# Gated linear attention and a squared-ReLU layer on one core: later chunks of 128 tokens handled in pairs

## The chip, the core and the metric

The kernel runs on one core of a Trainium2 chip. A core has a matrix engine (TensorE, PE in the profile, with its weight loads as PEld), VectorE (DVE), ScalarE (ACT), GpSimd (POOL) and SyncE (SP), which here only issues transfers, and 16 DMA engines. Each engine works through its own queue in order. PE and its helpers exchange data through PSUM (eight banks of 2 KB per partition) and SBUF. The metric is the device time of one execution in microseconds. The span in a profile runs from the first to the last instruction; the time of the execution is a little longer.

## The reference

```python
# q, k, v, alpha: (4, 8, 768, 48); w_in (384, 2048); w_out (2048, 384)
for t in range(S):
    state = alpha[:, :, t, :, None] * state + np.einsum('bhd,bhe->bhde', k[:, :, t], v[:, :, t])
    y[:, :, t] = np.einsum('bhd,bhde->bhe', q[:, :, t], state)
x = np.ascontiguousarray(y.transpose(0, 2, 1, 3)).reshape(B * S, H * D)      # 3072 x 384
h = x @ w_in
r = np.maximum(h, 0.0)
out = (r * r) @ w_out
```

## The kernel before

**Chunks.** The recurrence is computed in 24 chunks of 128 tokens, six to each of the four batch entries. With A the running product of alpha inside a chunk, a chunk needs the scores (q A)(k / A)^T under a triangular mask, the product of q A with the state that the chunks before left, and the new state. All eight heads of a chunk are worked on together, two heads (2 x 48 channels, padded to 2 x 64) on the 128 partitions.

**One chunk's steps.** ScalarE takes the logarithm of alpha (L396, tile L_s). PE sums it along the tokens with a triangular matrix (p0), ScalarE takes exponentials of the sum and of its negative. For chunks before number 11 DVE multiplies q and k by these in token order (L502, L505), PE transposes both products, and a copy brings them to SBUF. From chunk RAW = 11 on ("raw" chunks) the plain q and k are cast to bf16 on POOL (L413, tile rawb) and transposed by a DMA (L416, DMA_TRANSPOSE, tile rawt), one for q and one for k of each chunk, each over four blocks of 128 columns. PE then forms the running sum in transposed form too (pT, four matmuls L_s by the triangular matrix), ScalarE's exponentials of it (L451 into qkT, L454 into aiT) are multiplied by the transposed q and k on DVE (L507, L510). Then come the scores on PE (p2, tile sc: eight matmuls of 64 rows, two heads side by side in the two halves of the array), two masks on DVE (L561), the product with v and with the state (p3a, p3b), a cast on ScalarE (xn, L386), and a transpose of the chunk's output into xT_big (by PE and DVE, for chunks 18 to 22 by a DMA, L620).

**Feed-forward.** Tokens are taken in groups (4, 1, 1 and then nine groups of 2 chunks). The first layer (add_moe1) fills a bank with 512 columns, ScalarE applies ReLU (L676, tile r, 96 in all), DVE squares (L684, tile gT). The second layer (add_moe2) accumulates over 16 blocks; its result is copied to an output tile and stored. The first eight token tiles are held in SBUF (tile keep) and stored late by two large transfers; tiles 8 to 17 are stored by transfers that POOL issues (L772), the rest by SP.

**Order.** The order of all work is written by a planner inside the kernel. Each operation is an `Op` with an engine, a planned duration, dependencies, a priority, and `lat`, the time from its end until its result counts as there. `Plan.run` picks greedily by planned times, and the instructions of all engines are emitted in that order, so each engine's queue is fixed when the program is built. Loads are planned on one line called DMA, one after the other; transposing DMAs ("TR") also take time on that line (TLD) and count as landed TLAT later, and their `late` moves their place in SP's queue back. All loads and transposing DMAs are issued from SP's queue. A chunk may begin when the feed-forward has progressed far enough (`gate`, with LEAD).

**PSUM.** The scores have two banks of their own (sl_sc, tile sc), the state has one, and five banks serve the rest. The small steps of the chunks use banks 0 and 1 (GLA_BANKS), the first layer banks 2 to 4, the second layer banks 4 to 2.

The helpers `mm` (L240) and `tr` (L243) record all matmuls and transposes, so these two lines stand for most of PE's work, and tiles tell the steps apart. A tile `bank` is any of the five banks.

Of the kernel before, what the change touches and what calls it, by code (L numbers as in the profile page):

```python
# [38 lines left out]
class Op:  # L39


    def __init__(self, eng, dur, emit, deps=(), prio=0.0, takes=None, gives=None, lat=None, at=0.0):
        self.eng, self.dur, self.emit = eng, dur, emit
        self.deps = []
        for d in deps:
            if d is not None:
                d = d if isinstance(d, tuple) else (d, None)
                if d[0] is not None:
                    self.deps.append(d)
        self.prio = prio  # L50
        self.takes, self.gives, self.lat, self.at = takes, gives, lat, at
        self.start = self.done = None

# [5 lines left out]
class Plan:  # L59
# [13 lines left out]
    def ready(self, op):  # L73
        t = op.at
        slack = PE_SLACK if "PE" in op.durs else 0.0
        if slack and self.free.get("PE", 0.0) > PE_CALM:
            slack = 0.25
        for d, x in op.deps:
            if d.done is None:
                return None  # L80
            if x is None:
                t = max(t, d.done + (slack if d.eng != "PE" else 0.0))
            else:
                t = max(t, d.start + d.dur + x)
        if op.takes is not None:
            best = None
            for sl in op.takes:
                f = sl.free_at()
                if f is not None and (best is None or f < best):
                    best, op.slot = f, sl  # L90
            if best is None:
                return None
            t = max(t, best)
        return t

    def run(self, gate):
        free = self.free
        while any(self.pending.values()):
# [34 lines left out]
            if op.takes is not None:  # L133
                self.ready(op)
                op.slot.release.append(op.gives if op.gives is not None else op)
            self.order.append(op)
            self.on_pick(op)
# [4 lines left out]
def kernel(  # L142
# [13 lines left out]
    P = 128  # L156
# [40 lines left out]
    utri_b = consts.tile([P, 1, P], BF16)  # L197
    nc.gpsimd.tensor_copy(utri_b[:, 0, :], utri_f)
    JN, JP = 4, 32
    JW = P + JN - 1  # L200
# [29 lines left out]
    nc.vector.memset(ae_s, 0.0)  # L230
    xT_big = big.tile([P, KT, n_tok], BF16)
    gT_s = big.tile([P, FT, 2 * P], BF16, name="gT2", tag="gT2")
# [78 lines left out]
    EARLY = 4  # L311
    RAW = 11
    XTURN = (18, 23)
    TLD, TLAT, TLATE = 1.0, 4.0, 2.0
    NR = 3
    R = {}

    def raw_tiles():
        if R:
            return  # L320
        R["b"] = stage.tile([P, NR, 2, H, DP], BF16, name="rawb", tag="stage")
        nc.gpsimd.memset(R["b"][:, :, :, :, D:], 0.0)
        R["t"] = stage.tile([P, NR, 2, NP, P], BF16, name="rawt", tag="stage")
        R["i"] = stage.tile([P, 2, NP, P], BF16, name="aiT", tag="stage")

# [38 lines left out]
    def add_load(s, nm):  # L364
        d = C[s]
        b, c = divmod(s, NCH)

        def ld():
            if nm not in d:
                d[nm] = loads.tile([P, H, D], FP32, name=nm)  # L370
            pin(nc.sync.dma_start(out=d[nm], in_=SRC[nm][b, c]))
        prev = C[s - LB].get("use_" + nm) if s >= LB else None
        d["ld_" + nm] = add("DMA", LD if s < 4 else LD1, ld, prev, lat=2.0 if s < 4 else LAG if s < 6 else 2.4, at=0.6)

    def add_chunk(s):
        d = C[s]
        b, c = divmod(s, NCH)
# [30 lines left out]
        if raw:  # L408
            w, wz = s % NR, s % 2

            def e_rb(j, nm):
                raw_tiles()
                pin(nc.gpsimd.tensor_copy(R["b"][:, w, j, :, 0:D], d[nm]))  # L413

            def e_turn(j):
                pin(nc.sync.dma_start_transpose(out=R["t"][:, w, j], in_=R["b"][:, w, j].rearrange("p h d -> p (h d)")))  # L416
            rt = []
            for j, nm in enumerate(["qt", "kt"]):
                cb = add("POOL", 0.55, lambda j=j, nm=nm: e_rb(j, nm), d["ld_" + nm],
                         *([C[s - NR]["turn"][j]] if s >= RAW + NR else []), prio=-5.0)  # L420
                d["use_" + nm] = cb
                t_ = add("TR", TLD, lambda j=j: e_turn(j), cb, *([C[s - NR]["turned"][j]] if s >= RAW + NR else []), lat=TLAT)
                t_.late = TLATE
                rt.append(t_)
            d["turn"] = rt
        vb = d["use_vt"] = add("POOL", 0.55, e_vb, d["ld_vt"], old, prio=-5.0)
# [22 lines left out]
        def e_AT():  # L449
            d["qkT"] = work.tile([P, 2 * NP, P], BF16, name="qkT")  # L450
            pin(nc.scalar.activation(d["qkT"][:, NP:2 * NP, :], d["pmT"], AF.Exp))  # L451

# [25 lines left out]
        if raw:  # L478
# [9 lines left out]
            aiT = add("ACT", 0.48, e_AiT, pT, after(aT), *([C[s - 2]["turned"][1]] if s >= RAW + 2 else []), **g)  # L488
            pT.gives = aiT
            if not last:  # L490
                ae0 = add("ACT", 0.18, lambda: e_aeT(0), pT, after(aiT), **g)
# [14 lines left out]
        def e_qAT():  # L506
            pin(nc.vector.tensor_mul(d["qkT"][:, 0:NP, :], R["t"][:, w, 0], d["qkT"][:, NP:2 * NP, :]))  # L507

        def e_kiT():
            pin(nc.vector.tensor_mul(d["qkT"][:, NP:2 * NP, :], R["t"][:, w, 1], R["i"][:, wz]))  # L510
        if raw:
            if not last:
                mk = d["use_kt"] = add("DVE", 0.47, e_kI, ai, d["ld_kt"], old, **g)
            cp = add("DVE", 0.34, e_qAT, aT, rt[0], **g)
            cpk = add("DVE", 0.34, e_kiT, aiT, rt[1], cp, **g)
            d["turned"] = [cp, cpk]
        else:
            mq = d["use_qt"] = add("DVE", 0.47, e_qA, a_, d["ld_qt"], old, **g)
            mk = d["use_kt"] = add("DVE", 0.47, e_kI, ai, d["ld_kt"], old, **g)

        def e_p1q():
# [26 lines left out]

        def e_p2():
            sc = d["sc"] = ps_sc.tile([P, 2, NP, P], FP32, name="sc")  # L550
            t = d["qkT"]
            for p in range(NP):
                for hh in range(2):
                    sl = slice(64 * hh, 64 * hh + 64)
                    mm(sc[:, hh, p, :], lhsT=t[sl, NP + p, :], rhs=t[sl, p, :], start=True, stop=True)
        p2 = d["p2"] = plan.add(Op("PE", 0.42, e_p2, [cp, cpk], takes=[sl_sc], lat=0.10, **g))

        def e_sm(hh):
            if hh == 0:
                d["sm"] = work.tile([P, 2, NP, P], BF16, name="sm")  # L560
            pin(nc.vector.tensor_mul(d["sm"][:, hh], d["sc"][:, hh], utri_b.to_broadcast([P, NP, P])))  # L561
        sm0 = add("DVE", 0.6, lambda: e_sm(0), p2, **g)
        sm1 = add("DVE", 0.6, lambda: e_sm(1), p2, after(sm0), **g)
        p2.gives = sm1

        if not last:
# [51 lines left out]
        if XTURN[0] <= s < XTURN[1]:  # L618
            def e_xt():
                pin(nc.sync.dma_start_transpose(out=xT_big[:, :, s * P:(s + 1) * P], in_=d["xn"]))  # L620
            d["x"] = add("TR", 0.8, e_xt, xn, lat=TLAT)
            d["x"].late = 1.0
            d["end"] = xn
# [3 lines left out]
        def e_xT():  # L627
            cast(xT, xT_big[:, :, s * P:(s + 1) * P], d["px"])
        xT = add({"ACT": 0.36, "DVE": 0.27} if s < EARLY else "DVE", 0.27, e_xT, p4, prio=-9.0)
# [13 lines left out]
    POOL_OUT = (5, 18)  # L643
    HELD, HELD_AT = 8, 150.0
    KEEP, held_ev = {}, []
# [6 lines left out]
    def add_moe1(g, f0, before, lo=0, hi=None, per=1):  # L652
        hi = GN[g] if hi is None else hi
        t0, n = (GT[g] + lo) * P, (hi - lo) * P
        w = per * n
# [18 lines left out]
        def e_relu():  # L674
            box["r"] = rpool.tile([P, 512], BF16, name="r")
            pin(nc.scalar.activation(box["r"][:, 0:w], box["ph"][:, 0:w], AF.Relu))  # L676
        rl = add("ACT", 0.055 + w / 1190.0, e_relu, op, prio=RELU_PRIO if g > 1 else RELU_PRIO0)
# [47 lines left out]
    def add_moe2(g, tt, before, box, quarters, pools):  # L725
# [22 lines left out]
        def e_ev():  # L748
            if held:
                if t % 4 == 0:  # L750
                    KEEP[t // 4] = stage.tile([P, 4, d_model], FP32, name="keep", tag="stage")
                box["ob"] = KEEP[t // 4][:, t % 4, :]
# [32 lines left out]
    for d in DMA_ORDER + list(range(6, NT)):  # L785
# [12 lines left out]
        else:  # L798
            for nm, _ in srcs:
                if nm != "at":  # L800
                    add_load(d, nm)
                elif d <= 9:
                    add_load(d, nm)
                if nm == "at" and 9 <= d < NT - 1:
                    add_load(d + 1, nm)
            add_chunk(d)
# [26 lines left out]

    LEAD = 3.7

    def gate(op):
        s = getattr(op, "gla", None)
        if s is not None:
            return s <= LEAD + (prog["m1"] + prog["m2"]) / 5.12
        return True  # L840
# [60 lines left out]
```

## Time and profile before

| | us |
|---|---|
| median of three runs | 186.35 |
| the three runs | 184.03, 186.35, 187.1 |
| the profiled execution | 185.07 |
| its span | 183.4 |

In the profile, a group line gives line, engine, operation, tiles, shape and count, then busy time and the mean of one in ns, then the engine's idle time before these instructions and what ended it. Some groups that matter:

```profile
L240 PE MATMUL bank<-xT_big,w_in_b 128*128 128x256 bf16 (+2 forms) x636 | 76.6, 262 | 0.9 <-ACT r L676 0.7
L240 PE MATMUL bank<-w_out_b,gT 128*128 128x384 bf16 (+1 forms) x400 | 71.6, 320 | 0.5 <-DVE w_out_b L296 0.5
L676 ACT ACTIVATE r<-bank 128x512 bf16<-128x512 f32 x96 | 56.6, 606 | 11.3 <-PE bank L240 9.9
L561 DVE TENSOR_TENSOR sm<-sc,utri_b 128x512 bf16<-128x512 f32 x48 | 30.8, 684 | 5.9 <-PE sc L240 5.7
L386 ACT CAST xn<-bank 128x384 bf16<-128x384 f32 x24 | 11.6, 482 | 11.6 <-PE bank L240 11.5
L413 POOL CAST rawb<-qt 128x384 bf16<-128x384 f32 x13 | 7.4, 570 | 20.3 <-DMA qt<-in_q_dram 20.3
```

The duration of a matmul here is that of one from its issue to the modelled end of its pipeline; matmuls overlap, so the distance between starts is what one costs.

Busy time by stage (start and end of the stage, its length, busy us of PE, PEld, DVE, ACT and POOL with the count of instructions, granted clock, DMA share, GB/s):

```profile
60.00:80.00 20.00, 20.00 (x244) 16.19 (x241) 18.31 (x39) 16.60 (x39) 5.48 (x10) 1.00 0.96 174
80.00:100.00 20.00, 19.92 (x210) 14.79 (x209) 15.54 (x34) 14.98 (x35) 5.90 (x11) 1.00 1.00 176
100.00:120.00 20.00, 19.33 (x197) 14.24 (x196) 14.48 (x34) 15.84 (x37) 5.80 (x11) 1.00 0.90 180
120.00:140.00 20.00, 20.00 (x202) 14.09 (x199) 13.44 (x28) 14.52 (x35) 7.28 (x14) 1.00 0.91 189
140.00:160.00 20.00, 20.00 (x212) 15.18 (x211) 14.52 (x30) 14.75 (x34) 4.38 (x8) 1.00 0.88 200
160.00:183.40 23.40, 20.48 (x175) 15.41 (x172) 5.63 (x14) 9.78 (x19) 0.00 (x0) 1.00 0.14 52
```

Transposing DMAs and copies (tile, queue, count, KB each, median us from issue to landing):

```profile
qt<-in_q_dram SPq DMA_DIRECT2D x24, 192.0 KB, 4.0
rawt<-rawb SPq DMA_TRANSPOSE x26, 3.4
xT_big<-xn SPq DMA_TRANSPOSE x5, 2.5
```

### The profile page before, as it was taken

How to read it: one execution, taken by the hardware profiler on the slowest of the kernel's cores; microseconds unless marked ns; L12 is line 12 of the kernel's file. 1: busy time of each engine (PE TensorE's matmuls, PEld its weight loads, DVE VectorE, ACT ScalarE, POOL GpSimd, SP SyncE). 2: the span in 40 equal slices, each digit the busy share in tenths (PEclk: the TensorE clock that was granted, in tenths of full speed). 3: DMA queues.
4: the chain of work that ended last, by engine and by line, in shares of the span. 5: the costliest groups of instructions: out<-in, count | busy, mean ns of one | idle time of the engine just before them, and what ended most of it. 6: DMA issues, size and time to landing. Idle time of an engine off the chain costs nothing.

```text
span 183.4 us, 4946 instructions
## 1 busy us (share of the span) xinstructions
PE 177.5 (97%) x1908; PEld 130.5 (71%) x1908; DVE 127.1 (69%) x273; ACT 126.5 (69%) x286; POOL 39.4 (21%) x80
## 2 busy tenths in 40 slices
PE   7999999899999999999999998999999999999993
PEld 2577884567769877867768776667766777778663
DVE  1179898684999998778877867748855984744200
ACT  3677799226859996966967859847975895767321
POOL 8221100021131142132223133342323512000000
PEclk9999999999999999999999999999999999999999
DMA  5999999999999999998999599898898898901022
GB/s 168 215 212 252 302 366 321 326 220 204 177 191 201 194 179 173 141 190 161 150 193 202 113 240 186 161 227 162 170 201 182 176 163 194 301 13 43 12 77 86
DMA packets 120200, 34.12 MB, mean 186 GB/s; under 512 B 112400, under 2 KB 118928, under 8 KB 120176
## 3 DMA queue, kind: packets, MB, share of 16 engines
q1 hardware_dynamic: 119536, 31.83, 80.7%
q0 software_dynamic: 640, 1.97, 3.2%
q8 instruction: 15, 0.25, 0.6%
q14 instruction: 9, 0.07, 0.2%
HBM read 25.17 MB, written 4.72 MB: 163 GB/s over the span
## 4 chain that ended last, share of the span: by engine, by line
PE 49%; DMA 2%; ACT 1%; issue 0%; DVE 0%
PE bank L240 45%; DMA at<-in_alpha_dram 2%; PE sc L240 2%; PE st L240 1%; PE bank L243 1%; ACT aiT L454 0%; ACT r L676 0%; ACT ob L758 0%; ACT L_s L396 0%; ACT ob L716 0%; DVE xT_big L388 0%; ACT qkT L451 0%
## 5 line engine op out<-in xcount | busy, mean ns | idle before, releaser
L240 PE MATMUL bank<-xT_big,w_in_b 128*128 128x256 bf16 (+2 forms) x636 | 76.6, 262 | 0.9 <-ACT r L676 0.7
L240 PE MATMUL bank<-w_out_b,gT 128*128 128x384 bf16 (+1 forms) x400 | 71.6, 320 | 0.5 <-DVE w_out_b L296 0.5
L676 ACT ACTIVATE r<-bank 128x512 bf16<-128x512 f32 x96 | 56.6, 606 | 11.3 <-PE bank L240 9.9
L240 PEld LDWEIGHTS <-w_in_b 128*128 128x128 bf16 x636 | 52.7, 98 | 10.6 <-issue 1.5
L240 PEld LDWEIGHTS <-gT 128*128 128x128 bf16 x416 | 37.2, 98 | 18.7 <-DVE w_out_b L296 1.0
L684 DVE TENSOR_TENSOR gT<-r 128x512 bf16<-128x512 bf16 x96 | 41.8, 453 | 10.2 <-ACT r L676 9.0
L561 DVE TENSOR_TENSOR sm<-sc,utri_b 128x512 bf16<-128x512 f32 x48 | 30.8, 684 | 5.9 <-PE sc L240 5.7
L405 POOL CAST vb<-vt 128x384 bf16<-128x384 f32 x24 | 13.6, 569 | 69.1 <-DMA vt<-in_v_dram 55.2
L386 ACT CAST xn<-bank 128x384 bf16<-128x384 f32 x24 | 11.6, 482 | 11.6 <-PE bank L240 11.5
L505 DVE TENSOR_TENSOR kI_s<-kt,Ainv 128x384 bf16<-128x384 f32 x21 | 12.8, 611 | 7.8 <-ACT Ainv L466 7.8
L240 PEld LDWEIGHTS <-qkT 64*128 64x128 bf16 (+1 forms) x272 | 10.7, 95 | 6.4 <-issue 2.4
L586 ACT CAST sb<-st 128x384 bf16<-128x384 f32 x20 | 9.6, 482 | 7.7 <-DVE st L581 7.5
L758 ACT COPY ob<-bank 128x384 f32<-128x384 f32 x14 | 6.7, 480 | 8.0 <-PE bank L240 8.0
L396 ACT ACTIVATE L_s<-at 128x384 bf16<-128x384 f32 x20 | 10.5, 527 | 2.4 <-DMA at<-in_alpha_dram 2.3
L240 PE MATMUL bank<-warm 128*128 128x256 bf16 (+1 forms) x54 | 10.9, 348 | 1.3 <-DVE warm L188 1.3
L502 DVE TENSOR_TENSOR qA_s<-qt,A 128x384 bf16<-128x384 f32 x11 | 6.3, 575 | 8.0 <-ACT A L462 8.0
L413 POOL CAST rawb<-qt 128x384 bf16<-128x384 f32 x13 | 7.4, 570 | 20.3 <-DMA qt<-in_q_dram 20.3
L413 POOL CAST rawb<-kt 128x384 bf16<-128x384 f32 x13 | 7.6, 587 | 19.0 <-DMA kt<-in_k_dram 11.1
L581 DVE TENSOR_TENSOR st<-st,ae_s 128x384 f32<-128x384 f32 x20 | 11.1, 556 | 0.5 <-PE st L240 0.5
L466 ACT ACTIVATE Ainv<-bank 128x384 bf16<-128x384 f32 x21 | 10.5, 501 | 1.1 <-PE bank L240 1.0
L240 PE MATMUL sc<-qkT 64*128 64x128 bf16 x192 | 9.5, 219 | 0.0
L240 PEld LDWEIGHTS <-sm 128*128 128x128 bf16 x192 | 8.1, 96 | 1.7 <-issue 0.2
(64 smaller groups left out, 165.7 us busy)
## 6 DMA issues: line engine op xcount, KB each, us to landing
qt<-in_q_dram SPq DMA_DIRECT2D x24, 192.0 KB, 4.0
kt<-in_k_dram SPq DMA_DIRECT2D x24, 192.0 KB, 3.6
vt<-in_v_dram SPq DMA_DIRECT2D x24, 192.0 KB, 3.8
at<-in_alpha_dram SPq DMA_DIRECT2D x20, 192.0 KB, 4.0
wo<-in_moe_w_out_dram SPq DMA_DIRECT2D x4, 768.0 KB, 8.5
out_dram<-ob POOLq DMA_DIRECT2D x10, 192.0 KB, 3.1
wi<-in_moe_w_in_dram SPq DMA_DIRECT2D x4, 384.0 KB, 5.3
wi<-in_moe_w_in_dram SPq DMA_DIRECT2D x2, 768.0 KB, 8.3
```

The lines of the kernel that those rows point to most:

```text
L240: pin(nc.tensor.matmul(*a, **kw))
L386: pin(nc.scalar.copy(out_t, in_t))
L396: pin(nc.scalar.activation(L[:, :, 0:D], d["at"], AF.Ln))
L405: pin(nc.gpsimd.tensor_copy(d["vb"], d["vt"]))
L413: pin(nc.gpsimd.tensor_copy(R["b"][:, w, j, :, 0:D], d[nm]))
L466: pin(nc.scalar.activation(d["Ai"], d["pm"][:, 0:HD].rearrange("p (h d) -> p h d", h=H), AF.Exp, scale=-1.0))
L505: pin(nc.vector.tensor_mul(kI[:, :, 0:D], d["kt"], d["Ai"]))
L561: pin(nc.vector.tensor_mul(d["sm"][:, hh], d["sc"][:, hh], utri_b.to_broadcast([P, NP, P])))
L581: pin(nc.vector.tensor_mul(st4, st4, bcast(ae, D)))
L586: pin(nc.scalar.copy(d["sbt"], d["st"]))
L676: pin(nc.scalar.activation(box["r"][:, 0:w], box["ph"][:, 0:w], AF.Relu))
L684: pin(nc.vector.tensor_mul(gT[g][:, f0:f0 + per, lo * P:lo * P + n], r, r))
```

## The change

RAW goes from 11 to 10, so that chunks 10 to 23, seven pairs, are raw. From chunk 10 on (DUO = 10):

- q of two chunks is loaded by one transfer whose rows hold two neighbouring tokens (2 x 48 floats, 384 bytes instead of 192). Two POOL casts, one for the even and one for the odd tokens, and one transposing DMA over eight blocks follow. In each chunk of the pair the query tokens then stand even ones first, odd ones behind.
- k of the two chunks is loaded by two transfers as before and transposed by one DMA over eight blocks, after both casts.
- the exponential for q is written in the same interleaved order (L451 before, a read of its bank with a step of two), a second mask utri_q has that order, and the ReLU of the groups from chunk 10 on puts the tokens back, by reading its bank in the order a, i, r with r the slower half (neighbours 64 floats apart).
- the scores of both chunks are one operation of 16 matmuls on PE. The first chunk's scores go to banks 0 and 1, the second's to sc. The masks that follow release them (`holds`).
- the planner counts loads of alpha as landed 6.0 us after their planned time from chunk 11 on (2.4 before), other loads from chunk 12 on 3.8 (2.4), transposing DMAs 5.0 (4.0), those of xT 7.0 (4.0), and a transposing DMA's time on the DMA line is 2 x 0.8 for two chunks instead of 1.0 for one. The gate for paired chunks is 4.0 and 4.6 (plus 0.6 from chunk 16 on) instead of 3.7.
- xT_big becomes a ring of 12 chunks, q has its own tile q_s, and twelve token tiles instead of eight are held for late stores, so that POOL issues six output transfers instead of ten.

```diff
-    RAW = 11
+    RAW = 10
-    TLD, TLAT, TLATE = 1.0, 4.0, 2.0
+    DUO = 10
+    TLD, TLAT, TLATE = 0.8, 5.0, 2.0
+    ALATE, XLAT, LT = 6.0, 7.0, 3.8
...
-        d["ld_" + nm] = add("DMA", LD if s < 4 else LD1, ld, prev, lat=2.0 if s < 4 else LAG if s < 6 else 2.4, at=0.6)
+        d["ld_" + nm] = add("DMA", LD if s < 4 else LD1, ld, prev, lat=2.0 if s < 4 else LAG if s < 6 else ALATE if s > RAW and nm == "at" else 2.4 if s < RAW + 2 else LT, at=0.6)
+
+    def add_q_pair(s):
+        b, c = divmod(s, NCH)
+        src = q[b, :, c * P:(c + 2) * P, :].rearrange("h (p r) d -> p h (r d)", r=2)
+        Q = q_s[:, s // 2 % 3, :].rearrange("p (h rd) -> p h rd", h=H)
...
+        ld = d["ld_qt"] = add("DMA", 1.6, lambda: pin(nc.sync.dma_start(out=Q, in_=src)), *old, lat=LT if s > RAW else 2.4, at=0.6)
+        def e_rb(r):
+            raw_tiles()
+            pin(nc.gpsimd.tensor_copy(R["qb"][:, w, r, :, 0:D], Q.rearrange("p h (r d) -> p h r d", r=2)[:, :, r, :]))
+        def e_turn():
+            pin(nc.sync.dma_start_transpose(out=R["qt"][:, w].rearrange("p r n t -> p (r n) t"),
+                                            in_=R["qb"][:, w].rearrange("p r h d -> p (r h d)")))
...
+        d["qturn"] = add("TR", 2 * TLD, e_turn, *d["use_q"], ..., lat=TLAT)
+    def add_scores(*pair):
+        def dst(s):
+            d = C[s]
+            if len(pair) == 2 and s == pair[0]:
+                d["sc"] = [banks[sl.bank].tile([P, NP, P], FP32, name=f"bank{sl.bank}") for sl in GLA_BANKS]
+            else:
+                t = ps_sc.tile([P, 2, NP, P], FP32, name="sc")
+                d["sc"] = [t[:, hh] for hh in range(2)]
+        def e_p2():
+            for s in pair:
+                dst(s)
+                t = C[s]["qkT"]
+                for p in range(NP):
+                    for hh in range(2):
+                        sl = slice(64 * hh, 64 * hh + 64)
+                        mm(C[s]["sc"][hh][:, p, :], lhsT=t[sl, NP + p, :], rhs=t[sl, p, :], start=True, stop=True)
+        mask = utri_q if pair[0] >= RAW else utri_b
...
+        p2 = plan.add(Op("PE", 0.18 + 0.24 * len(pair), e_p2, [o for s in pair for o in C[s]["cps"]], lat=0.10, **g))
+        for s in pair:
+            d = C[s]
+            d["p2"] = p2
+            sm0 = add("DVE", 0.6, lambda d=d: e_sm(d, 0), p2, prio=-10.0 + s * 0.01)
+            sm1 = add("DVE", 0.6, lambda d=d: e_sm(d, 1), p2, after(sm0), prio=-10.0 + s * 0.01)
+            d["sms"] = [sm0, sm1]
+            p2.holds += [(sl_sc, sm1)] if s == pair[-1] else list(zip(GLA_BANKS, [sm0, sm1]))
...
-            pin(nc.scalar.activation(d["qkT"][:, NP:2 * NP, :], d["pmT"], AF.Exp))
+            pin(nc.scalar.activation(d["qkT"][:, NP:2 * NP, :].rearrange("p n (r i) -> p n r i", r=2),
+                                     d["pmT"].rearrange("p n (i r) -> p n r i", r=2), AF.Exp))
...
-            d["x"] = add("TR", 0.8, e_xt, xn, lat=TLAT)
-            d["x"].late = 1.0
+            d["x"] = add("TR", 0.8, e_xt, xn, lat=XLAT)
+            d["x"].late = 1.8
...
-    HELD, HELD_AT = 8, 150.0
+    HELD, HELD_AT = 12, 152.0
...
-            pin(nc.scalar.activation(box["r"][:, 0:w], box["ph"][:, 0:w], AF.Relu))
+            o, x = box["r"][:, 0:w], box["ph"][:, 0:w]
+            if GT[g] >= RAW:
+                o = o.rearrange("p (a i r) -> p a i r", i=DP, r=2)
+                x = x.rearrange("p (a r i) -> p a i r", i=DP, r=2)
+            pin(nc.scalar.activation(o, x, AF.Relu))
...
+    MORE = 0.6
+    DUO_LEAD = 4.0, 4.6
-            return s <= LEAD + (prog["m1"] + prog["m2"]) / 5.12
+            return s <= (LEAD if s < DUO else DUO_LEAD[s % 2] + (MORE if s >= 16 else 0.0)) + (prog["m1"] + prog["m2"]) / 5.12
```

## The prediction

> **What bounds the kernel now.** I read the page's busy shares and slices first.
>
> ```profile
> PE 177.5 (97%) x1908; PEld 130.5 (71%) x1908; DVE 127.1 (69%) x273; ACT 126.5 (69%) x286; POOL 39.4 (21%) x80
> ...
> PE   7999999899999999999999998999999999999993
> ...
> DMA  5999999999999999998999599898898898901022
> ```
>
> TensorE (PE) works in nearly every slice, at full granted clock. Less time can only come from fewer or denser matmuls, or from the few places where PE stands still. The DMA engines are nearly as busy until about 155 us, so a late load is the likely cause of such a place. The chain of waits shows one:
>
> ```profile
> 105.20 0.07 PE bank L240
> 105.28 4.13 DMA at<-in_alpha_dram
> ...
> 109.42 0.34 ACT L_s L396
> ...
> 110.42 0.28 issue
> 110.70 0.60 ACT aiT L454
> 111.30 0.49 ACT r L676
> 111.79 0.04 issue
> 111.84 0.49 PE bank L240 x3
> ```
>
> A load of alpha lands at 109.40; the logarithm (L396) stands at the head of ScalarE's queue and waits for it; an output copy, two exponentials and the ReLU queue behind. In PE's timeline the ReLU comes too late for the next first-layer matmul:
>
> ```profile
> 108.89 2.29 PE L240 MATMUL bank<-xT_big,w_in_b 128*128 128x256 bf16 x18
> 111.84 0.49 PE L240 MATMUL bank<-xT_big,w_in_b 128*128 128x256 bf16 x3 [0.66 <-ACT r L676]
> ```
>
> By the starts of the single matmuls in the trace, two steps here take 0.273 and 0.929 us where 256 columns take 0.107: 0.17 + 0.82 = 0.99 us lost. The other losses between 60 and 160 us are small (0.23 at 82.9, 0.18 at 94.9, 0.10 at 103.9) and follow DVE instructions that ran long.
>
> Last, the scores in PE's timeline:
>
> ```profile
> 118.59 0.65 PE L240 MATMUL bank<-w_out_b,gT 128*128 128x384 bf16 x3
> 119.17 0.40 PE L240 MATMUL sc<-qkT 64*128 64x128 bf16 x8
> 119.50 0.34 PE L240 MATMUL bank<-w_out_b,gT 128*128 128x384 bf16 x1
> ```
>
> The eight start at 119.175, .179, .242, .245, .298, .301, .354 and .357, in twos that run together every 0.056 us, and the next matmul starts at 119.505. The first comes 0.258 us after a 384-column matmul that needs 0.160: 0.098 us to get in. The step out takes 0.148, where a further two would start after 0.053: 0.095 to get out. Every burst in the trace shows both.
>
> **The change, part by part.**
>
> *Scores in pairs.* A burst of 8 costs 0.098 + 0.330 = 0.43 us, two 0.86. A burst of 16 adds four twos to one burst: 0.43 + 4 x 0.056 = 0.65. Saved 0.205 us a pair; the built order has seven bursts of 16 where fourteen of 8 were. All of it is PE's own time: **-1.43 us**.
>
> *Chunk 10 takes the way of the later chunks.* By starts on PE, it loses four one-column matmuls (4 x 0.026) and eight transposes (8 x 0.058) and gains four L_s matmuls (4 x 0.061): 0.57 - 0.24 = **-0.32 us**. ScalarE trades one exponential of 0.49 for two of 0.61 (+0.73), DVE 0.58 + 0.69 for 0.46 + 0.44 (-0.37), POOL gets two casts (+1.14). In slices with DVE and ScalarE at 70 to 90% PE's queued matmuls hide this; uncovered, it would be the 0.73.
>
> *Alpha planned later.* The planner now counts 6.0 us after the load's own time instead of 2.4, from chunk 11 on, so logarithms stand further back in ScalarE's queue. From there on these loads land 2.9 to 4.5 us after their issue, and those of chunks 13, 14, 15, 19 and 23 end 0.02 us before the logarithm starts: it waited. 3.6 us more clears all that the trace shows. Gain: the stall at 110, **-0.99 us**. What is late next: the transposed k, whose least margin (landing to use) was 2.7 us; q's was 2.3 to 8.5.
>
> *DMA results planned later, fewer DMAs.* On SP's queue a pair now costs seven copies and two transposing DMAs, where it was eight and four. In this stretch a copy issues in 0.57 us and about 0.06 passes between: 7 x 0.63 = 4.4 us. For eight blocks of 128 columns instead of four the trace has no row. Lower bound: issue does not grow (least 1.19 for four blocks, 1.21 for the three of xT). Upper: double the median 1.52, 3.0. So a pair costs 6.8 to 10.4 us of SP, against PE's pace: scores of chunk 10 start at 71.85, those of 23 at 158.54, 6.67 a chunk, 13.3 a pair. SP is ahead either way; I take 2.0, between. The order puts six copies between the pair's q load and its transposing DMA: 3.8 us of issue, which covers the 2.7 to 4 us to landing. Packets of 192 bytes took 15.8 ns and those of 256, 21.7, so the q pair's 1024 of 384 bytes, at an estimated 25 to 30, take 16 engines 1.6 to 1.9 us where 2048 took 2.0. Effect on the end: 0.
>
> What SP must not do is wait at a transposing DMA, since loads are queued behind it. It does now:
>
> ```profile
> SPq L416 <- POOL rawb L413: 11.1, 10, 1.7
> SPq L416 <- POOL vb L405: 9.9, 8, 2.0
> ```
>
> 21 us in all, for POOL casts. The change bundles six casts a pair (3.4 us on POOL, as before) but takes four output issues (0.56 us each, and their waits for ScalarE) off POOL's queue, since twelve token tiles are held instead of eight. The third held store goes out when the DMA share is 0.14. No cost; uncovered, a wait of 2 us on SP would eat margin, not yet PE time.
>
> *The waits that the pair adds.* The burst waits for both chunks' products on DVE; behind those stand squares (L684) and masks. Four masks now follow each other, 4 x 0.68 = 2.7 us; the squares queue behind them, but ScalarE frees PE's banks and eight r tiles hold 8 x 0.6 us of first-layer results. Both GLA banks are taken until the first two masks end, 1.4 us in which PE has only feed-forward matmuls, of which it always holds a group. Casts on POOL slow the DVE instruction beside them (0.76 instead of 0.42 at 82.1), and they now come in a row. Bounds: 0, as covered, to 0.5 us, what the three small losses sum to now; I take **+0.2 us**.
>
> *Interleaved tokens.* Chunks from 10 on hold even tokens first, then odd. Each ReLU of their groups (7 groups x 8 = 56) now reads its bank with neighbours 64 floats apart, and 14 exponentials (L451) with a step of two floats. Nearest rows, reads of a bank without and with a step:
>
> ```profile
> L469 ACT ACTIVATE ae_s<-bank x7: 163/169/190, 31.9 to 68.9; 64x4 f32<-64x4 f32 x7
> L458 ACT ACTIVATE ae_s<-bank x20: 162/170/209, 82.0 to 151.0; 64x4 f32<-64x4 f32 x20
> L359 ACT ACTIVATE ae_s<-bank x2: 181/187/193, 13.0 to 13.2; 64x16 f32<-64x16 f32 x2
> ```
>
> L458 steps 128 floats per element, L469 none: 170 against 169. L359 steps four floats: 18 ns for 12 more elements, 1.5 each, between the 0.97 of contiguous reads ((606 - 482) / 128, ReLU against xn) and twice that. Bounds: 0 and 512 x 0.97 = 0.50 us each. I take 0, by L458, whose step is the nearer one. [...]
>
> **Sum.** -1.43 - 0.32 - 0.99 + 0.2 = -2.5 us. The profiled execution took 185.07 (span 183.4, 1.7 around it): 182.5. It lies below the middle of the four times shown (184.03, 185.07, 186.35, 187.1: 185.7); on that scale **183.1 us**. Forecast's own range 182 to 184.8.
>
> **Rivals.**
>
> *More stalls go.* Two runs took 1.3 and 2.0 us longer than the profiled execution; if that is late loads too, margin saves it, and the three small losses (0.5): 185.07 - 2.7 - 0.5 = 181.8 or a little less. For: the margins near zero. Against: the small losses come from DVE. 20%.
>
> *The wait moves to k.* A pair's k is transposed only once its second chunk has landed and been cast. If that reaches SP late and one transposing DMA takes over 4.4 us ((13.3 - 4.4) / 2), SP sets the pace. For: one of four blocks took 3.48 with its wait. Against: median 1.52. At 0.4 us a pair, 7 x 0.4 = 2.8 eats the gain: 185.7. 16%.
>
> *The burst does not merge.* PE pays the way in and out between the two chunks too: 183.1 + 1.4 = 184.5. Against: twos of one burst follow evenly although weights change each time. 7%.
>
> *Slower: strided reads.* If each element read across a step costs double, 70 instructions x 0.50 = 35 us more on ScalarE. From 80 to 160 us ScalarE is busy 14.98 + 15.84 + 14.52 + 14.75 = 60.1 of 80; about 29 of the 35 fall there on 19.9 idle, and the rest hits the last groups. PE then waits for banks: 7 to 15 us more, 190 to 198, say 192. It decides from 19.9 / 70 = 0.28 us each. For: L359. Against: L458. 10%.
>
> **Numbers.** Forecast 47%, rivals 20, 16, 7 and 10. Two per cent of 186.35, about what a measurement of this kernel can tell from no change, is 3.7 us: faster below 182.6, slower above 190.1. Faster: 17 of the first rival's 20 and 22 of the forecast's 47, 39%. Slower: the last rival and 3 of the second, 13%. Same 48%. Range 180.8 to 187.5: it takes in a second rival twice as dear on one side and the first with all its terms on the other, and leaves out the strided case and thin ends, about 17%.
>
> **What would show it.** Seven bursts of 16 with 0.10 and 0.095 at the ends and 0.056 between; no wait of L396 on alpha from chunk 11 on; r on ScalarE still 0.6 us; transposing DMAs below 3 us on SP; no PE gap before scores. Wrong if r rises above 0.88 us, if scores wait for DVE's products of k, or if alpha still stops ScalarE.

## The result and the profile after

| | kernel before | changed kernel |
|---|---|---|
| median of 18 runs each, us | 185.0 | 183.22 |
| lowest and highest | 183.56, 189.98 | 182.11, 185.06 |
| the profiled execution | 185.07 (span 183.4) | 183.37 (span 181.7) |

The ratio is 0.9907, with an interval of 0.9879 to 0.9936: the changed kernel is faster by 1.2 to 0.6%, less than 2%. The forecast was 183.1 us and "within 2%" its likeliest outcome. The prediction's working, however, gave 2.5 us of gain; what came is 1.7. The ratio is taken over fast runs alone, without those more than 1.5% above the fastest of their kernel, and 0.93% of 185.0 is 1.7 us where the medians of the table differ by 1.8. The rest of this document is about where those 0.8 us were counted wrongly.

In the changed kernel the lines are renumbered: `mm` is L252 (L240 before), the logarithm L493 (L396), the ReLU L774 (L676), the exponential for q L546 (L451), the masks L461 (L561), the products with the transposed q and k L606 and L609 (L507, L510), the transposing DMA of q L418 and that of k L513 (both L416 before).

The page first: busy shares, and the busy tenths of PE and the DMA engines.

```profile
PE 175.0 (96%) x1899; PEld 130.5 (72%) x1900; DVE 124.5 (69%) x273; ACT 126.4 (70%) x287; POOL 39.6 (22%) x80
...
PE   7999999899969999999999999999999999999993
...
DMA  5999999999899898989999999799997202970212
```

PE is busy 2.5 us less (177.5 before; durations overlap, so this is not yet time) and is still what bounds the kernel. The one low slice, the 6, lies at 50 us, far ahead of everything that the change touches; it is read below.

A double burst of scores in PE's timeline (start, duration, engine, line, tiles, shapes, count):

```profile
109.97 0.81 PE L252 MATMUL bank<-w_out_b,gT 128*128 128x384 bf16 x4
110.72 0.40 PE L252 MATMUL bank<-qkT 64*128 64x128 bf16 x8
110.95 0.39 PE L252 MATMUL sc<-qkT 64*128 64x128 bf16 x8
111.27 1.16 PE L252 MATMUL bank<-xT_big,w_in_b 128*128 128x256 bf16 x9
```

The second eight start 0.23 us after the first, where a lone burst is followed by its successor after 0.33. By the starts of the single matmuls the last one ahead begins at 110.458 and needs 0.160; the burst begins at 110.716 (way in 0.098), runs in twos every 0.056 across the border between the two chunks (110.893, 110.949, 111.005), and the next matmul starts at 111.268, 0.148 after the last two. From the end of the matmul ahead to the one behind, all seven double bursts take 0.65 us; a single one takes 0.427. Saved: 2 x 0.427 - 0.651 = 0.203 us a pair.

The groups that the rivals spoke of (busy us, mean ns, idle before):

```profile
L774 ACT ACTIVATE r<-bank 128x512 bf16<-128x512 f32 x96 | 55.5, 610 | 6.3 <-PE bank L252 5.0
L461 DVE TENSOR_TENSOR sm<-bank,utri_q 128x512 bf16<-128x512 f32 x14 | 9.0, 684 | 2.6 <-PE bank L252 2.6
L546 ACT ACTIVATE qkT<-bank 128x512 bf16<-128x512 f32 x14 | 8.4, 600 | 1.8 <-PE bank L252 1.6
```

The ReLU went from 606 to 610 ns, although 56 of its 96 now read with neighbours 64 floats apart, and the exponential with a step of two from 612 to 600. The transposing DMAs, by queue time (least, median, most, in ns):

```profile
L418 SPq DMA_TRANSPOSE rawt<-rawb x7: 1383/2060/2847, 66.1 to 133.0; - x7
L513 SPq DMA_TRANSPOSE aiT<-rawt x4: 1251/1420/2446, 68.8 to 134.7; - x4
L513 SPq DMA_TRANSPOSE aiT<-rawb x3: 1251/1255/1276, 81.2 to 124.7; - x3
```

All are below 3 us. What SP waited for at these lines:

```profile
SPq L418 <- POOL vb L502: 5.7, 5, 2.4
SPq L513 <- POOL vb L502: 3.1, 4, 0.9
SPq L418 <- POOL rawt L510: 1.7, 1, 1.7
SPq L513 <- POOL rawt L510: 0.2, 1, 0.2
```

That is 10.7 us in place of 21. And the stall at 110 us is gone: loads of alpha from chunk 11 on land 3.1 to 11.5 us ahead of their logarithm. But the chain of waits of this execution shows its twin at another place:

```profile
45.33 4.95 DMA at<-in_alpha_dram
50.28 0.02 issue
50.30 0.52 ACT L_s L493
50.82 0.37 ACT keep L856
51.19 0.39 ACT xn L483
51.58 0.04 issue
51.62 0.91 PE bank L252 x8
```

The alpha of chunk 7 lands at 50.28, the logarithm waits for it, an output copy and a cast queue behind, and PE stands for about 1.4 us before 51.62. In the profiled execution of before the same load landed 1.55 us ahead of its use. Nothing in the diff changes chunk 7. So each of the two profiled executions has one late alpha that stops PE, at different places, and the question is what such a lateness belongs to: the kernel, or the execution.

### The profile page after: what moved, and what is told of

It is laid out like the page before. It is cut to its first block, busy times and chain, and to the rows that moved or that the text cites. A ratio compares the mean times of both kernels' runs of the same rounds, so it can differ in the third digit from the quotient of the medians.

```text
span 181.7 us, 4874 instructions
## 1 busy us (share of the span) xinstructions
PE 175.0 (96%) x1899; PEld 130.5 (72%) x1900; DVE 124.5 (69%) x273; ACT 126.4 (70%) x287; POOL 39.6 (22%) x80
## 4 chain that ended last, share of the span: by engine, by line
PE 76%; DMA 9%; ACT 5%; SPq 4%; DVE 2%; issue 1%; POOL 0%; POOLq 0%; ACTq 0%
PE bank L252 69%; DMA wi<-in_moe_w_in_dram 5%; SPq L400 4%; PE bank L255 3%; DMA at<-in_alpha_dram 3%; ACT r L774 2%; PE sc L252 2%; DMA vt<-in_v_dram 2%; PE st L252 1%; DVE gT L782 1%; DVE w_in_b L308 1%; ACT Ainv L562 0%; ACT aiT L550 0%; ACT keep L856 0%; POOL vb L502 0%
## 5 line engine op out<-in xcount | busy, mean ns | idle before, releaser
L252 PE MATMUL bank<-xT_big,w_in_b 128*128 128x256 bf16 (+2 forms) x635 | 73.4, 262 | 0.2
L252 PE MATMUL bank<-w_out_b,gT 128*128 128x384 bf16 (+1 forms) x400 | 70.7, 320 | 0.5 <-DVE w_out_b L308 0.5
L252 PEld LDWEIGHTS <-w_in_b 128*128 128x128 bf16 x636 | 53.8, 98 | 9.4 <-issue 0.6
L774 ACT ACTIVATE r<-bank 128x512 bf16<-128x512 f32 x96 | 55.5, 610 | 6.3 <-PE bank L252 5.0
L782 DVE TENSOR_TENSOR gT<-r 128x512 bf16<-128x512 bf16 x96 | 40.1, 440 | 17.0 <-ACT r L774 15.5
L252 PEld LDWEIGHTS <-gT 128*128 128x128 bf16 x416 | 37.1, 98 | 19.4 <-DVE w_out_b L308 1.0
L415 POOL CAST rawb<-q_s 128x384 bf16<-128x384 f32 x14 | 8.8, 656 | 28.5 <-DMA q_s<-in_q_dram 28.5
L461 DVE TENSOR_TENSOR sm<-sc,utri_b 128x512 bf16<-128x512 f32 x20 | 12.8, 684 | 1.5 <-PE sc L252 1.4
L252 PEld LDWEIGHTS <-qkT 64*128 64x128 bf16 (+1 forms) x272 | 10.5, 95 | 4.4 <-issue 2.2
L856 ACT COPY ob<-bank 128x384 f32<-128x384 f32 x9 | 4.3, 479 | 12.6 <-PE bank L252 12.4
L252 PE MATMUL bank<-warm 128*128 128x256 bf16 (+1 forms) x54 | 10.9, 348 | 1.3 <-DVE warm L196 1.3
L493 ACT ACTIVATE L_s<-at 128x384 bf16<-128x384 f32 x20 | 10.4, 527 | 2.2 <-DMA at<-in_alpha_dram 2.2
L599 DVE TENSOR_TENSOR qA_s<-q_s,A 128x384 bf16<-128x384 f32 x10 | 5.5, 553 | 9.0 <-ACT A L558 9.0
L461 DVE TENSOR_TENSOR sm<-bank,utri_q 128x512 bf16<-128x512 f32 x14 | 9.0, 684 | 2.6 <-PE bank L252 2.6
L546 ACT ACTIVATE qkT<-bank 128x512 bf16<-128x512 f32 x14 | 8.4, 600 | 1.8 <-PE bank L252 1.6
L870 POOL DMA_DIRECT2D out_dram<-ob x6 | 3.4, 567 | 26.7 <-ACT ob L856 19.5
```

The lines of the kernel that those rows point to most:

```text
L252: pin(nc.tensor.matmul(*a, **kw))
L415: pin(nc.gpsimd.tensor_copy(R["qb"][:, w, r, :, 0:D], Q.rearrange("p h (r d) -> p h r d", r=2)[:, :, r, :]))
L461: pin(nc.vector.tensor_mul(d["sm"][:, hh], d["sc"][hh], mask.to_broadcast([P, NP, P])))
L493: pin(nc.scalar.activation(L[:, :, 0:D], d["at"], AF.Ln))
L774: pin(nc.scalar.activation(o, x, AF.Relu))
L782: pin(nc.vector.tensor_mul(gT[g][:, f0:f0 + per, lo * P:lo * P + n], r, r))
```

## The experiments

Theory A: PE's own saving (bursts, chunk 10) is the gain; waits for alpha are an accident of single executions, so the 0.99 us at 110 us were never in the median. Theory B: the late alphas belong to the order of the kernel, the one at 110 us was taken away, and the one at 50 us is its price. Rivals for the bursts: PE's saving lies partly under other waits, so that it does not all reach the end.

To compare executions, one stretch is worked out from the starts of the matmuls: from the first matmul of the second layer (32 to 33 us) to the last start on PE. It is 147.6 us in the profile of before and 145.7 in that of the changed kernel.

**The changed kernel, again.** No edit.

> The changed kernel, profiled once more. Theory A (lateness of early loads varies from execution to execution): the 1.4 us in which PE waited at 50 us behind the logarithm of chunk 7 is there in another size or not at all, the span is 180.2 to 181.8. Theory B (the change itself makes the loads of 35 to 50 us late): the same wait of 1.2 to 1.6 us is there again. In both: seven bursts of 16 scores with 0.10 and 0.095 us at their ends, and no wait over 0.3 us on PE from 65 us to the end.

One execution: 183.71 us, with a span of 182.0, a little over the range of theory A. The alpha of chunk 7 now lands 1.55 us ahead of its logarithm. PE still loses 0.24 us at this place, but so it does in the second profile of the kernel before (0.23 at 50.3 us), also without a wait for alpha. Instead one burst of chunk 9, which is no pair, stands; the expectation had no such wait after 65 us:

```profile
63.00 2.00 DVE L782 TENSOR_TENSOR gT<-r 128x512 bf16<-128x512 bf16 x3
63.39 1.33 POOL L510 CAST rawt<-kt 128x384 bf16<-128x384 f32 x2
64.93 0.68 DVE L485 COPY qkT<-bank 128x1024 bf16<-128x1024 bf16 x1
65.66 0.40 PE L252 MATMUL sc<-qkT 64*128 64x128 bf16 x8 [0.81 <-DVE qkT L485]
```

The three squares ahead of the copy took 2.00 us beside the casts of chunks 10 and 11 on POOL. In the first profile of the changed kernel, where POOL was idle at this time, they took 1.09 and the burst did not wait:

```profile
63.62 1.09 DVE L782 TENSOR_TENSOR gT<-r 128x512 bf16<-128x512 bf16 x3
```

The stretch on PE is 145.6 us. The wait for alpha at 50 us does not come back in each execution of this kernel, so it does not explain what is missing from the gain.

**A break in the double burst, and its control.** One matmul of a single column over all 128 rows, whose column is overwritten by the scores, is put between the two chunks' scores, or, as the control (`pair[0]` in the edit instead of `pair[1]`), ahead of both.

```diff
         def e_p2():
             for s in pair:
                 dst(s)
+                if len(pair) == 2 and s == pair[1]:
+                    mm(C[s]["sc"][0][:, 0, 0:1], lhsT=warm[:, 0:P], rhs=ones_col, start=True, stop=True)
```

> The changed kernel with one matmul of 128 rows and one column between the two chunks' scores of each pair, so that PE leaves the 64-row form and enters it again. If the way in and out is what pairing saved: each pair takes 0.20 to 0.23 us longer, 7 x 0.22 = 1.5 us in all, ratio to the changed kernel 1.008, to the kernel before about 0.999. Rival (the gain comes only from waits that went away): under 0.3 us, ratio to the kernel before 0.991 to 0.992.

> Control: the same seven extra matmuls, but ahead of the first chunk's scores, where PE changes its form anyway. Both theories: 7 x 0.026 = 0.2 us more than the changed kernel, ratio to the kernel before 0.991 to 0.993. If it costs as much as the one between, the extra matmul itself is dear and the other run shows nothing.

On PE the bursts now cost 0.427 + 0.440 = 0.867 us instead of 0.651, in the control 0.651 to 0.653 as without the extra matmul:

```profile
74.06 0.40 PE L252 MATMUL bank<-qkT 64*128 64x128 bf16 x8
74.39 0.18 PE L252 MATMUL sc<-ones_t,warm 128*128 128x1 bf16 x1
74.50 0.40 PE L252 MATMUL sc<-qkT 64*128 64x128 bf16 x8
```

The second eight start 0.44 us after the first, not 0.23. Seven times 0.216 is 1.51 us. In time, though: ratio to before 0.9981 (0.9955 to 1.0008) with the break and 0.9953 (0.9925 to 0.998) in the control, a difference of 0.28%, 0.5 us, give or take 0.7. The ratio with the break is the 0.999 that was expected, within its interval, but the control lies above its range (0.991 to 0.993). The difference has the expected direction and a third of the expected size, and these intervals do not tell it from nothing.

**Three breaks.** Since one break left open how much of PE's time reaches the end, the dose was trebled: a break after the 4th, 8th and 12th matmul.

```diff
                 for p in range(NP):
+                    if len(pair) == 2 and (p == 2 or p == 0 and s == pair[1]):
+                        mm(C[s]["sc"][0][:, p, 0:1], lhsT=warm[:, 0:P], rhs=ones_col, start=True, stop=True)
```

> The changed kernel with three matmuls of one column on all 128 rows in each double burst of scores, after its 4th, 8th and 12th matmul, so that PE leaves and enters the half-array form three times more. On PE a burst should take 0.651 + 3 x 0.216 = 1.30 us, seven bursts 4.5 us more. The run with one such matmul (1.51 us on PE) came out only 0.28% behind its control. Theory full: what the scores cost PE is the kernel's time, one for one; then 4.5 us, 2.4% more than the changed kernel, a ratio near 1.02 to the kernel before, and the small difference of the run with one matmul was scatter. Theory partly hidden: some other thing (loads, masks) sets the pace in this stretch and PE has slack there; then clearly less, a ratio of 1.00 to 1.01.

Each burst takes 1.30 us on PE, as expected, seven of them 4.5 us more. The ratio is 1.0152 (1.0122 to 1.0182), against 0.9949 (0.9913 to 0.9986) of the changed kernel, which was measured on another chip (the run after the next): 2.03%, 3.7 us, give or take 0.9. The stretch on PE went to 149.1 us, from 144.9 to 145.7 in three profiles of the changed kernel. So most of what the scores cost PE is the kernel's time. Both doses together, weighted by their intervals, give 1.1 us, give or take 0.3, for each 1.5 us on PE: about three quarters, an estimate, which takes it that time put into a burst acts like time taken out. Where the rest goes is not shown. That "full" holds is not excluded by the three breaks; the one break speaks against it (0.5 us, give or take 0.7, where it asks for 1.5).

**Chunk 10 alone.** The kernel before with `RAW = 10` and nothing else.

> The kernel before with RAW = 10 instead of 11 and nothing else, so that chunk 10 alone takes the way of the later chunks. By the prediction's sum 0.32 us less on PE (ratio 0.998), with the waits on alpha as before or worse, since two transposing DMAs more lie on SP's queue: 0.996 to 1.004. Rival (the gain is mostly chunk 10's): 0.991 to 0.994.

Ratio 1.0027 (0.9999 to 1.0056). The four one-column matmuls and eight transposes are gone, yet nothing is gained; the middle of the interval is a loss of 0.5 us. The rival, that the gain is mostly chunk 10's, falls. Its profile has no wait at 110 us, but a burst that stands 0.10 us longer, one of chunk 9 that waits 0.50 for its product, and 2.90 us from the end of the last output copy to the end of the span, where before has 2.53. One profile can't say which of these comes back in each run. The wait of chunk 9 is the one of the changed kernel's second profile: three squares beside chunk 10's casts (1.70 us). Of the eleven profiles here of kernels with `RAW = 10`, four have it (0.47 to 0.88 us of PE), those in which such casts fall beside the squares; of the three with `RAW = 11`, none. So, as far as these profiles show, it is a price of chunk 10's way that some executions pay.

**The changed kernel beside single parts.** The changed kernel without an edit, on the same chip as three of the runs below (alpha planned later alone, pairs without later planning, alpha a whole chunk ahead):

> The changed kernel beside the next three on one chip, so that they can be compared directly. Ratio to the kernel before 0.989 to 0.995. If lateness varies from execution to execution, this profile has PE waits of 0.5 to 2.5 us in all between 32 us and the end, most of them before 65 us.

Ratio 0.9949 (0.9913 to 0.9986), median 183.22; the stretch on PE 144.9 us. Single steps (over 0.05 us, those at the scores apart) lose 1.65 us from 33 us on, within the range, but only 0.67 of it before 65 us, not most.

**Only alpha planned later.** The kernel before, with 6.0 instead of 2.4 us for alpha from chunk 11 on:

```diff
-... LAG if s < 6 else 2.4, at=0.6)
+... LAG if s < 6 else 6.0 if s > 10 and nm == "at" else 2.4, at=0.6)
```

> The kernel before with one planning constant changed: alpha of chunks 11 on counts as landed 6.0 us after its load's time instead of 2.4. Theory A (the stall of 0.99 us at 110 us is one execution's, and most executions lose less there): ratio 0.996 to 1.000; the trace has no wait of a logarithm on alpha after 65 us. Theory B (the stall is there in nearly every execution and the later planning removes it): 0.993 to 0.995.

Ratio 1.001 (0.9984 to 1.0037): nothing. No wait for alpha is left on ScalarE after the first loads, and the first-layer matmuls that were stopped at 110 us run through:

```profile
108.63 0.39 PE L240 MATMUL bank<-utri_b,L_s 128*128 128x128 bf16 x4
108.85 2.48 PE L240 MATMUL bank<-xT_big,w_in_b 128*128 128x256 bf16 x21
111.26 0.40 PE L240 MATMUL sc<-qkT 64*128 64x128 bf16 x8
```

**The kernel before, again.** The last test of the 0.99 us.

> The kernel before, once more, with a profile. If the 0.99 us that PE lost at 110 us was this one execution's late load, as the two runs of single parts say, there is no step over 0.5 us between 100 and 120 us, and from the first second-layer matmul to the last start on PE it takes 146.3 to 146.9 us instead of 147.6. If the stall belongs to the order of the kernel before, the logarithm of the chunk at 110 us waits again and 147.6 comes back.

184.25 us. With the order untouched, the wait is not there either:

```profile
108.70 0.52 ACT L396 ACTIVATE L_s<-at 128x384 bf16<-128x384 f32 x1
108.76 0.39 PE L240 MATMUL bank<-utri_b,L_s 128*128 128x128 bf16 x4
...
108.98 2.61 PE L240 MATMUL bank<-xT_big,w_in_b 128*128 128x256 bf16 x21
```

The logarithm has no wait behind its line, and the 21 matmuls lose 0.16 us in all, not 0.99. The stretch on PE takes 146.5 us instead of 147.6. Of the four profiles of kernels that plan alpha as the kernel before does (two of that kernel, chunk 10 alone, and the pairs of the next run) only the first shows the stall, and the 1.4 us at 50 us are in one of all fourteen. On these chips theory B falls: the order does not bring the lateness in every execution. The first comparison is another session, though: its 18 runs of before go up to 189.98 us, the 81 later ones, on three chips, lie between 183.21 and 185.91. Whether late loads were commoner there is not shown.

**Pairs, but nothing planned later.** The changed kernel with the planner's old figures.

```diff
-    TLD, TLAT, TLATE = 0.8, 5.0, 2.0
-    ALATE, XLAT, LT = 6.0, 7.0, 3.8
+    TLD, TLAT, TLATE = 0.8, 4.0, 2.0
+    ALATE, XLAT, LT = 2.4, 4.0, 2.4
...
-            d["x"].late = 1.8
+            d["x"].late = 1.0
```

> The changed kernel with the older landing times of the planner (alpha 2.4, other loads 2.4, transposing DMAs 4.0, xT 4.0), so that only the pairs are left. Theory A: the pairs' saving on PE stays, 0 to 0.6 us of waits come back, ratio to the changed kernel 1.000 to 1.004. Theory B: the margins of 3 to 7 us that alpha has in the changed kernel are needed, one to three waits of 0.5 us or more come back after 65 us, and the ratio is 1.005 to 1.010.

Ratio 0.9968 (0.9943 to 0.9992): without the later planning, the rest of the change still makes the kernel faster, as theory A said. Against the whole change (0.9949) the difference of 0.2% is within the scatter. Its profile loses 1.4 us to single steps on PE between 65 and 90 us, where three profiles of the changed kernel lose 0.1 to 0.3; so the later planning may be worth something together with the pairs, which the times do not show.

**Eight held tiles.** The changed kernel with `HELD, HELD_AT = 8, 150.0`, so that POOL issues ten output transfers again.

> The changed kernel with eight held token tiles as before (stored from 150 us) instead of twelve: four more transfers are issued from POOL's queue, between the casts of q, k and v. The prediction took the four fewer as the cover for the bundled casts, and said that a wait on SP would eat margin, not PE time. If that holds: the ratio to the kernel before stays at 0.993 to 0.999, and SP's waits for POOL's casts grow from 10.7 us. If POOL's queue is what the pairs hang on: PE gaps ahead of double bursts and a ratio over 1.00.

Ratio 0.9979 (0.9946 to 1.0011), in the range for "holds". The waits of SP at its transposing DMAs grew, with L418 alone to 15.8 us. The profile also shows what the prediction had not listed, PE standing inside a double burst:

```profile
121.76 0.54 POOL L870 DMA_DIRECT2D out_dram<-ob  x1 [1.04 <-DVE ob L854]
...
122.05 1.49 DVE L609 TENSOR_TENSOR qkT<-aiT 128x512 bf16<-128x512 bf16 x1
...
122.29 0.52 POOL L510 CAST rawb<-kt 128x384 bf16<-128x384 f32 x1
...
122.74 0.51 POOL L502 CAST vb<-vt 128x384 bf16<-128x384 f32 x1
...
123.59 0.40 PE L252 MATMUL sc<-qkT 64*128 64x128 bf16 x8 [0.55 <-DVE qkT L609]
```

The multiply that makes the second chunk's k has a median of 0.42 us in the changed kernel and took 1.49 here, from 122.05 to 123.53, while POOL had an output's issue and two casts with next to no pause until 123.25. The burst took 1.37 us instead of 0.65. Where the multiplies of this shape run beside an output's issue alone, they take at most 0.43 us (34 in the fourteen profiles), so it is the casts that fit, and the extra issues on POOL can matter by moving casts beside a multiply. That they did so here is a reading of one execution; the times (0.3% behind the changed kernel) don't tell it from scatter.

**Alpha earlier for chunks 7 to 9.** Two attempts at the wait at 50 us. First, alpha loaded a whole chunk ahead from chunk 7 on instead of 10:

```diff
-                elif d <= 9:
+                elif d <= 6:
...
-                if nm == "at" and 9 <= d < NT - 1:
+                if nm == "at" and 6 <= d < NT - 1:
```

> The changed kernel with alpha of chunks 7 to 9 loaded one chunk ahead, as from chunk 10 on already. The wait for alpha of chunk 7 near 50 us (1.4 us of PE in the first profile of the changed kernel, 0.25 in the second) cannot be there; q, k and v of those chunks come 1 us later, and the planned order has a gap of 0.5 us for it near 49 us. If the wait is common: ratio to the changed kernel 0.995 to 0.999. If it is rare: 1.000 to 1.003.

Ratio 1.005 (1.0026 to 1.0074): slower than both kernels, 1% behind the changed one on the same chip, and outside both ranges that were expected. The planner answers with another order, and in it two places on PE stand:

```profile
77.51 0.33 PE L252 MATMUL bank<-sb,qkT 128*128 128x96 bf16 x4 [1.17 <-DVE sm L461]
...
137.85 0.40 PE L252 MATMUL sc<-qkT 64*128 64x128 bf16 x8 [0.94 <-DVE qkT L609]
```

The first is the price of the pair that the prediction bounded: both small banks hold the first chunk's scores until DVE has masked them, and PE has nothing else ready. The masks stood behind four squares that took 2.65 us beside POOL's casts. Second, each of these loads moved ahead of only one other:

```diff
-                if nm == "at" and 9 <= d < NT - 1:
-                    add_load(d + 1, nm)
+                if nm == "kt" and 6 <= d < 9 or nm == "at" and 9 <= d < NT - 1:
+                    add_load(d + 1, "at")
```

> The changed kernel with the loads of alpha of chunks 7 to 9 each moved ahead of one load (the v of the chunk before), so that they land earlier; in the order written out by the kernel nothing else moves by much, unlike in the run with alpha a whole chunk ahead, in which one double burst stood 1.1 us. If the wait for an early alpha (0.2 to 1.55 us at 50 us) is worth time in most executions: the wait at 50 us is gone in the profile and the ratio to the kernel before is 0.990 to 0.995, below the changed kernel's 0.9949. If the loads are simply all late in that stretch, another load takes the place of alpha: the ratio stays at 0.995 or rises.

Ratio 0.9927 (0.9899 to 0.9955), median of six 182.56. That is the lowest ratio of the experiments, but it can't be told from the changed kernel: the intervals overlap, and they are from two chips. The step at 50 us still loses 0.35 us, no less than in two of the three profiles of the changed kernel (0.24), although alpha landed 1.25 us ahead here and 1.55 and 1.65 in those two: what is left of this step is no wait for alpha, so the edit had little to remove. It is no shown improvement.

## Why the prediction was right, and where it was not

**The total** was right (183.1 predicted, 183.22 measured), and partly for a wrong reason. The sum took 2.5 us off an execution with a stall, and set it beside a middle of 185.7 from four runs. With 18 runs that middle is 185.0; the gain is 1.7 us. Too large a gain and too high a start cancelled, by luck.

**Bursts, -1.43 us.** The mechanism and the size on PE were right to 0.002 us a pair: the way in and out of the 64-row form (0.098 and 0.095 us) is paid once per burst, though the weights change with each matmul (a two every 0.056 us). What failed is the sentence "All of it is PE's own time" as a statement about the end: by the breaks about three quarters of PE's time there reaches it, some 1.1 us (estimate).

**Chunk 10, -0.32 us.** The work did leave PE, but alone it gave a ratio of 1.0027. The prediction's other end, 0.73 us of ScalarE uncovered, is nearer to that in size, but what the profiles show is DVE: the wait of chunk 9's burst behind squares that chunk 10's casts slowed, 0.57 us in this run's profile and present in four of eleven. That this is all is not shown: the end of the kernel is longer too in this profile, by 0.37 us.

**Alpha planned later, -0.99 us: the step that failed.** The stall was measured rightly and is real, in that one execution. It was then booked as a property of the kernel, and on the later chips it is none. The step measured 0.1% the other way when done alone (interval -0.16 to +0.37%), and the wait is missing from a second profile of the same kernel. The prediction had noted what should have warned: loads of five chunks ended 0.02 us before their logarithm, but only one of them cost PE more than 0.25 us.

**Clusters of masks and casts, +0.2 us.** The size is not shown. From 65 to 160 us, where the change acts, the second profile of before loses 0.59 us in single steps over 0.05 us (those at the scores apart), three profiles of the changed kernel 0.45, 0.77 and 0.98: the difference is from -0.14 to +0.39 us, no clearer than one execution from the next. The mechanism is there, casts on POOL that slow DVE and so hold up PE (chunk 9's three squares took 2.00 us beside casts and 1.09 without), but its dearest places lie above the 0.5 us that was the upper bound: chunk 9's burst, 0.88 us in one of those three profiles, and 1.17 us in the run with alpha a chunk ahead.

**SP and the DMAs, 0.** Right. Eight blocks issue in 1.25 us at least, four in 1.19, but the 14 issues of the first profile run up to 2.85 and have a mean of 1.82, near the 2.0 that was taken. The q pair's packets of 384 bytes took 24.2 ns, a little under the 25 estimated. SP waits half as long for POOL (10.7 us, 21 before). The held tiles that the prediction named as cover are not shown to be needed by the times, though the run with eight has a burst that waits.

**Rivals.** "More stalls go" asked for 181.8 or less and did not come; nor is a stall found that the order brings in each execution. "The wait moves to k" shows itself only in variants (0.94 and 0.55 us before L609), and by DVE running late, not SP. The burst merges. "Strided reads" fell: 610 ns, where 0.28 us more would have been needed to decide; the last 56 ReLUs alone, which read with a step, have a median of 598 ns, and the 40 ahead of them too.

What stays open: whether the whole gain is nearer to the 1.7 us of the first comparison or to the 0.9 of the second (0.9949 of 183.92), whose intervals overlap, and whether late loads in the first session make up the difference; how much of chunk 10's saving is lost to the wait of chunk 9's burst; and what lengthens the end of the kernel a little (2.67 us from the end of the last output copy to the end of the span, in two profiles, where before has 2.53 and 2.55).

## What to carry to other kernels

A stall seen in one profile is first looked for in a second profile of the same kernel; only what comes back may be booked as gain, and here a second profile would have taken 1 us out of the sum. Time that is PE's own work in every execution, such as the way in and out of the 64-row form (0.098 and 0.095 us a burst here), is the safer promise, and even of that a part may go into slack: a control that puts the cost back in two doses tells how much arrives. Moving a load a whole chunk ahead in a hand-tuned order changes much more than the load, so a change of place is best made by one position and read on PE's timeline.

## What the runs showed of the hardware

- A single one-column matmul over all rows, put among matmuls of 64 rows, cost 0.216 us a burst (0.867 in place of 0.651; with three of them 1.30), nearly all of it the way out and in again (0.095 + 0.098). Put ahead of the burst, it left the burst at 0.651 to 0.653.
- Two matmuls of 64 rows, side by side in the array, ran on without a gap when the target bank changed from one tile to another in the middle of the burst: in all seven double bursts of the first profile of the changed kernel the first two behind the border start 0.055 to 0.056 us after the last two ahead of it, as within a chunk.
- The transposing DMA's shortest issue hardly grew with the number of blocks (least 1.19 us for four, 1.25 for eight). The median of all issues is 1.52 us for four in the first profile of before, and for eight in that of the changed kernel 2.06 (q) and 1.27 (k). It landed 1.8 us (median) after the issue's end for four blocks and 1.9 to 2.0 for eight in these two profiles; single ones took up to 4.5.
- A bf16 multiply of 128x512 on DVE took at most 0.43 us wherever no cast ran on POOL beside it (1264 in the fourteen profiles). Of the 466 that a cast touched, 204 took over 0.60 us, most of these 0.7 to 0.8, and one took 1.49 us, beside two casts without a pause.
